# A fixed sequence of operations in place of a planner, and pairs of units in the second half of an attention kernel

## The chip, the cores and the metric

The kernel runs on one core of a Trainium2 chip. The metric is the device time of one execution in microseconds; the kernel before takes 975.54 us (median of 3 runs, 974.77 to 976.95). TensorE (PE) multiplies matrices, VectorE (DVE), ScalarE (ACT) and GpSimd (POOL) work on elements, and SyncE (SP) issues the DMAs.

## What is computed

A causal attention with a cumulative bias is followed by two feed-forward layers. All tensors are float32; the data of q and k are scaled by 8 before the call, which changes no shape.

```python
B, H, S, D = 4, 8, 576, 64
scores = q @ k.T / sqrt(D)                       # causal
bias   = -(cum[:, :, :, None] - cum[:, :, None, :])   # cum = cumsum(max(s, 0))
attn   = softmax(scores + minimum(bias, 0)) @ v
x = attn.transpose(0, 2, 1, 3).reshape(B * S, H * D)          # 2304 x 512
h = x @ moe_w_in                                 # 512 -> 2048
x = (h - tanh(h)) @ moe_w_out                    # -> 512
x = ((x @ moe2_w_a) * (x @ moe2_w_b)) @ moe2_w_out   # 512 -> 1536 -> 512
```

## The kernel before, in words

Precision comes from splitting each float32 factor into a high and a low 16-bit part; every such matrix is scaled by a power of two first, which needs its norm. So an operand of a product is loaded, squared and summed (ACT), summed over the partitions by a product with ones (PE), turned into a power of two by a handful of one- to three-column operations (DVE, `pow2`), and then split into hi (a scaled copy) and lo (the scaled difference).

**Attention.** A *unit* is one batch, one pair of heads and one half of the queries. The first half (`u.merged` false) holds the query tiles 0 and 1 of 128 rows. The second half (`u.merged` true, 16 units) holds tiles 2 and 3 and the last 64 rows, the *tail*; the tails of the two heads share one tile. A unit goes through `g_load` (raw q, k, v into SBUF, DMAs on SP), `u_load` (bias rows into `kB`), `g_square`, `g_scale`, `g_split` (v), `u_split` (q and k into tile `qk`), `u_turn` (one DMA transpose of `qk` into `qkT`, then copies into `kB`, `qB`, `qkT`), the products q·k, the exponentials, and the products with v. In the first half several units share a group `g` and so a load, a scale and a split of v; in the second half each unit is its own group. Its tile `raw` has two buffers (`BUFS_R`), `qk` one, `v` three.

**The layers.** Rows go through the first layer in 8 blocks of 256 rows and one tail block: per block eight tiles `h`, then `g` and its hi and lo (`ghl`), and a sum in `acc`. Its blocks run between attention units, since each needs finished attention rows. The second layer comes last, from about 650 us of the profile on; most of its blocks use seven products in place of eight, with sums of half tiles before them (`sq<-sq`, `g<-g`, `w<-sq,g`, 128x256).

**What sets the order.** The program records every operation with what it depends on, and the engines on which it may run (`either`: DVE, ACT or POOL). `follow` gives each operation a due time, decoded from the string `ORDER`. `run` then simulates the engines with a table of costs (`cost`), issues what is ready and due first, and picks the engine that would be done first. A POOL instruction that reads two tiles waits for the DVE instruction of that sort which was issued last before it. Nearly every instruction passes one helper, so all have the line L651 (L635 in the changed kernel); tiles tell them apart.

Of the kernel before, what the change touches and what calls it, by code (L numbers as in the profile page):

```python
# [38 lines left out]
    "Ibs7IAzUIANqIAOkIAOKIAPbIARiIATLIAU6IAWOIAsGIAV6IAUdIAaJIAeJIAlVIAoSIAbpIAdbIAezIAh4IAjWIAgtIAe4IAelIAPWIARyIAOHIATBIAUP"  # L39
    "IAQlIAOQIAUiIAVuIAYeIAZnIAbxIAePIAcrIAXFIARtIAYLIARJIAaCIAZ/IAGLIAgTIAmpIAVyIAZgIAZDIAX8IAUmIAm8IAkOIAjbIAklIApsIApXIApQ"  # L40
    "IAlhIAhBIAoeIAoHIAnoIAuBIA1YIAqJIAu1IA88IAp9IAn7IAiFIAkOIAo/IAqPIAl5IAkPIArzIAweIAqfIAv6IBCUIA2yIBL0IAtNIAiGIAqhIAsqIAwa"
    "IAm+IArHIA05IAz0IAyLIAzdIAydIA3+IA8dIA/pIBBrIBCuIBAxIBCFIBPCIBFqIBHkIBHoIA7JIA78IBHlIA5dIA6sIA5eIBBuIBEPIBDxIBMCIBF/IBFO"
    "IBHdIBTNIBSuIAg3IAc2IAbnIAeVIAeyIAf6IAd6IAZWIAUrIAceIAdHIAYwIAh0IAh+IAiDIAlCIAmSIAsLIAt6IAm9IArnIAobIAv3IAl/IAn2IApVIAlD"
    "IAs2IAxvIBBhIBAMIBFqIBI3IA2eIBDxIA4LIBBlIBBrIA8YIBDQIBFEIBHRIBFTIBJzIBWZIBElIBJ2IBDnIBDpIBECIBEDIBGUIBIcIBIbIBPNIBKrIBMS"
    "IBZKIBa7IBcNIAxeIA3MIBFKIAzrIA84IA+HIBA1IBGPIA92IBF5IBIFIBMvIBNJIBR/IBPjIBLzIBLNIBT8IBTZIBFOIBSBIBPmIBQ4IBTUIBRYIBOLIBP9"
    "IBPYIBQOIBRiIBWRIBYXIBZIIBD0IBWpIBWrIBdJIB2XIEPgIEf8IEPZID9jICmLICq+ICVJICaLICZ1ICWlICdoIAx8IA2KIA4tIA62IAw4IBG9IBLLIBMa"
    "IApPIAwtIA0vIBDYIBS+IBenIBfpIB8wIBbfIBWWIBhaIBjRIBc6IB/IIB7fIB9uIBeCIB0yIBzkIB+tIB01IB7fIB+CICGeIBz0ICDpICExICLcICR2ICXs"
    "ICZuIClOICXKICjpICniIC0xIB6FICHoICWfIC8+ICK7ICg9ICcPIC6+IC+KIDKZIDNDIDPXIDBjIDRGIDUzIDWaIDWiIDXTIDZyIDdNIBOuIBm3IBhCIBgN"
    "IBgpIBzBIBuiIBy5IBQ5IBp4IBUqIBoEIBiuIBktIB4eICAeIB0pICBEIB5/IB/2ICIMICJzICOJICGjICHjICNEICLNICPoICLeICMiICcVICgrICVCICZZ"
    "ICWdICoaICxZICytICr2IC7PIC+dIC/RIDAuIDDwIDElIDHtIDONIDSBIDIXIDMFIDJkIDKOIDQiIDTQIDY+IDcvIDeCIDe/IDiRIDj7IDltIDmIIEA0IDln"  # L50
# [12 lines left out]
    "IEDOIEFiID7jID97ID7MID5vID+tIEIiIEKxIESLIEJNIEKgIEBtIEIPIEGGIEHRIEGRIERqIEVcIEVqIEaKIEgeIEQaIEZvIEQsIEVkIEcqIElzIEhyIEnQ"
    "IEkTIEiXIEXpIEdcIEY7IEc3IEk+IEopIEoCIEsXIEzTIE6qIEqoIErZIEuUIEw5IEywIE3xIE5vIE+xIE/lIFDAIE3yIFBzIE8pIFBPIFN5IFNrIFOuIFSt"
    "IFXLIFhhIFGEIFHvIFMfIFORIFaaIFYaIFXiIFcmIFdJIFoJIFahIFVYIFW3IFXiIFZGIbptIFcLIFclIFWnIFagIF+EIClDICeUICr4ICt5IC1IIC5BICt4"
    "IC4uIDCAIDRQIDTDIDUNIDW9IDVuIDW6IDZvIDcHIDb6IDgwIDbFIDb+IDn3IDCVIDbBIDhRIDYWIDiCIDenIDhBIDqYIDp0IDsxIDw/ID03ID2/IDwZID2G"
# [144 lines left out]
AHEAD = 20e3  # L211
# [125 lines left out]
class Plan:  # L337
# [133 lines left out]
    def follow(self, order):  # L471

        if 4 * len(self.ops) != len(order):
            return
# [1349 lines left out]
```

## Time and profile before

| what | value |
|---|---|
| median of 3 runs | 975.54 us |
| profiled execution | 976.21 us |
| its span | 974.4 us (1.8 us lie around it) |
| mean granted clock of TensorE | 0.991 |
| PE busy | 897.3 us, 92% |
| DVE busy | 787.2 us, 81%, 2056 instructions |
| ACT busy | 553.3 us, 57%, 1118 instructions |
| POOL busy | 180.4 us, 19%, 297 instructions |

Busy time is the union of the instructions on an engine; a stage that is bound by an engine shows it busy nearly all of the stage. The stages used below are the stretches between the first products of certain blocks: up to 41 us nothing of the first layer can run, from 130 us on attention and the first layer run interleaved, the second half of the queries is loaded from 202 us on, and from 650 us on the second layer runs alone.

### The profile page before, as it was taken

The page shows a single profiled execution, that of the slowest core. Times are in us where ns is not written, and L with a number is a line of the kernel's source. Part 1 is how long each engine was busy: PE and PEld are TensorE (multiplying, and loading weights), DVE is VectorE, ACT ScalarE, POOL GpSimd, SP SyncE. Part 2 cuts the span into 40 slices and gives each one's busy share as a digit, 9 for nine tenths or more (in the row PEclk, how much of TensorE's full clock was granted, in tenths as well). Part 3 has the DMA queues.
Part 4 walks back from the last instruction along what each step waited for, and adds up shares of the span by engine and source line. Part 5 has one row for each costly group of instructions (what it writes and reads, how often), then busy time and mean ns, then how long its engine had stood idle before and what let it go on. Part 6 is the DMA issues. An engine that isn't in the chain of part 4 may idle for free.

```text
span 974.4 us, 19580 instructions
## 1 busy us (share of the span) xinstructions
PE 897.3 (92%) x7304; PEld 617.2 (63%) x7304; DVE 787.2 (81%) x2056; ACT 553.3 (57%) x1118; POOL 180.4 (19%) x297
## 2 busy tenths in 40 slices
PE   1587988999998999999989999999999999999998
PEld 0354656666565656666656677686777777777774
DVE  8999998969999999998899999994585466466454
ACT  6888776748778788787798854431222122222220
POOL 2123122304344343322000022020020001000000
PEclk9998989999999999999999999999999999999999
DMA  8999964458999888888755410100020011000001
GB/s 227 190 296 246 219 129 84 97 100 156 167 180 180 165 177 159 183 167 140 273 195 194 152 44 23 44 1 23 10 79 2 1 44 45 1 1 17 28 1 44
DMA packets 262304, 109.16 MB, mean 112 GB/s; under 512 B 235264, under 2 KB 243696, under 8 KB 262208
## 3 DMA queue, kind: packets, MB, share of 16 engines
q1 hardware_dynamic: 262208, 107.90, 48.2%
q8 instruction: 57, 0.93, 0.4%
q14 instruction: 39, 0.32, 0.1%
HBM read 55.81 MB, written 11.17 MB: 69 GB/s over the span
## 4 chain that ended last, share of the span: by engine, by line
PE 51%; DVE 14%; DMA 6%; ACT 5%; issue 3%; SPq 2%; POOL 0%; ACTq 0%; DVEq 0%; POOLq 0%
PE h L651 16%; PE qk L651 14%; PE acc L651 13%; PE pv L651 8%; DMA qkT<-qk 3%; SPq L651 2%; DVE qk L651 2%; DVE a L651 2%; DVE ghl L651 1%; DVE w L651 1%; DVE h L651 1%; DMA raw<-in_k_dram 1%; DVE xf L651 1%; DVE z L651 1%; ACT sq L651 1%
## 5 line engine op out<-in xcount | busy, mean ns | idle before, releaser
L651 PEld LDWEIGHTS <-w 128*128 128x128 f16 x3840 | 372.0, 98 | 81.2 <-issue 9.5
L651 PE MATMUL h<-xhl,w 128*128 128x256 f16 x2256 | 280.9, 273 | 8.0 <-DVE ghl L651 2.6
L651 PE MATMUL acc<-w,ghl 128*128 128x512 f16 x984 | 234.4, 380 | 4.7 <-DVE ghl L651 3.1
L651 PEld LDWEIGHTS <-ghl 128*128 128x128 f16 x1128 | 108.2, 98 | 121.6 <-DVE ghl L651 7.0
L651 PE MATMUL h<-xf,w 128*128 128x256 f16 (+1 forms) x416 | 71.8, 311 | 0.0
L651 DVE CUSTOM_DVE_ANT_0 qk<-qk,caus,cs 128x128 f32<-128x128 f32 (+3 forms) x120 | 64.8, 554 | 2.5 <-PE qk L651 2.4
L651 ACT ACTIVATE g<-h 128x512 f32<-128x512 f32 x38 | 22.4, 596 | 66.0 <-PE h L651 63.7
L651 PE MATMUL qk<-qkT 128*128 128x128 f16 (+4 forms) x168 | 45.8, 316 | 13.8 <-DVE qkT L651 6.0
L651 DVE TENSOR_TENSOR sq<-sq 128x256 f32<-128x256 f32 x44 | 18.6, 422 | 47.3 <-ACT sq L651 47.3
L651 PE MATMUL pv<-xf,w 128*128 128x256 f16 x432 | 55.3, 273 | 1.3 <-DVE xf L651 0.9
L651 PE MATMUL qk<-xf,w 128*128 128x256 f16 x432 | 54.8, 273 | 0.0
L651 ACT ACTIVATE th<-h,xc 128x512 f32<-128x512 f32 x64 | 43.8, 685 | 15.4 <-PE h L651 13.1
L651 ACT ACTIVATE w<-w 128x1024 f32<-128x1024 f32 (+1 forms) x42 | 47.8, 1167 | 2.4 <-DMA w<-in_moe_w_out_dram 2.1
L651 PEld LDWEIGHTS <-sq 128*128 128x128 f16 x288 | 28.2, 98 | 31.0
L651 PEld LDWEIGHTS <-v 128*64 128x64 f16 x1440 | 37.9, 112 | 13.9 <-issue 12.4
L651 PE MATMUL qk<-kB,qB 67*128 67x128 f16 (+4 forms) x168 | 45.5, 314 | 0.0
L651 PEld LDWEIGHTS <-qkT 128*128 128x128 f16 (+1 forms) x176 | 16.7, 102 | 41.1 <-DVE qkT L651 17.0
L651 ACT ACTIVATE sq<-pv 128x512 f32<-128x512 f32 x24 | 14.3, 597 | 49.2 <-PE pv L651 49.0
L651 ACT ACTIVATE w<-h,cpc 128x256 f32<-128x256 f32 x24 | 11.3, 473 | 53.2 <-PE h L651 53.1
L651 DVE TENSOR_TENSOR g<-g 128x256 f32<-128x256 f32 x48 | 19.7, 429 | 26.9 <-ACT g L651 26.7
L651 ACT ACTIVATE sq<-raw 128x576 bf16<-128x576 f32 (+2 forms) x57 | 38.4, 675 | 5.2 <-DMA raw<-in_q_dram 2.4
L651 PE MATMUL pv<-aT,v 128*64 128x128 f16 x960 | 35.0, 224 | 4.4 <-DMA aT<-a 2.7
(267 smaller groups left out, 1728.1 us busy)
## 6 DMA issues: line engine op xcount, KB each, us to landing
w<-in_moe_w_out_dram SPq DMA_DIRECT2D x8, 1024.0 KB
w<-in_moe_w_in_dram SPq DMA_DIRECT2D x6, 1024.0 KB
x_d<-sq SPq DMA_DIRECT2D x9, 512.0 KB
w<-in_moe_w_a_dram SPq DMA_DIRECT2D x4, 1024.0 KB
out_dram<-x2f SPq DMA_DIRECT2D x16, 256.0 KB
ws<-in_moe_w_out_dram SPq DMA_DIRECT2D x3, 1024.0 KB
xf<-in_moe_w_b_dram SPq DMA_DIRECT2D x3, 1024.0 KB
w<-in_moe_w_b_dram SPq DMA_DIRECT2D x3, 1024.0 KB
```

The costliest lines, as they stand in the source:

```text
L651: return getattr(getattr(plan.nc, name), what)(*[real(a) for a in args], **{k: real(a) for k, a in kw.items()})
```

## The change

It does two things. `ORDER` no longer holds due times but the finished sequence: three characters for each operation, its index and the number of the engine that it runs on. A new function `emit` issues the operations in that sequence, with the same rule between POOL and DVE, and the simulation isn't run. (Two constants of the cost table are changed too; `emit` doesn't read them.)

Second, the units of the second half form pairs. `raw` gives way to `rawq`, `rawk` and `rawv`, each of one buffer for two units; `v` has two buffers of a pair in place of three of a unit. The loads of a pair are 11 DMAs in place of 18, each of twice the size. Norm, ones product and `pow2` are made once for a pair, so two units share their scales. The hi parts of q and k and both parts of v are written for the pair by one instruction each; the lo parts of q and k, the transpose and all that follows stay by unit. The tail rows move between the heads in the tiles (`wq`, `wk`, `qat`).

```diff
 ORDER = (
-    "Ibs7IAzUIANqIAOkIAOKIAPbIARiIATLIAU6IAWOIAsGIAV6IAUdIAaJIAeJIAlVIAoSIAbpIAdbIAezIAh4IAjWIAgtIAe4IAelIAPWIARyIAOHIATBIAUP"
...
-BUFS_R = {"raw": 2, "qk": 1, "z": 1, "inv": 4, "v": 3, "a": 3, "am": 1, "aTm": 1}
+BUFS_R = {"rawq": 1, "rawk": 1, "rawv": 1, "qk": 1, "z": 1, "inv": 4, "v": 2, "a": 3, "am": 1, "aTm": 1}
...
     def follow(self, order):
-        if 4 * len(self.ops) != len(order):
-            return
-        for op in self.ops:
-            t = base64.b64decode(order[4 * op.seq:4 * op.seq + 4])
-            op.dl = 8.0 * (int.from_bytes(t, "big") - (1 << 21))
+        if 3 * len(self.ops) == len(order):
+            n = [A64.index(c) for c in order]
+            n = [n[i] << 12 | n[i + 1] << 6 | n[i + 2] for i in range(0, len(n), 3)]
+            self.steps = [(self.ops[i >> 2], i & 3) for i in n]
+
+    def emit(self, switch):
+        if not self.steps:
+            return self.run(switch)
+        self.begin()
+        for op, way in self.steps:
+            assert all(p.wait < 0 for p in op.pred)
+            op.wait = -1
+            op.eng, op.fn, op.dur, op.lag = op.alts[way]
...
+            made = op.fn()
+            if op.fn.lock and op.eng == "vector":
+                self.turn = made
+            elif op.fn.lock and self.turn is not None:
+                self.after(made, self.turn)
...
-            if u.merged or p % (PAIRS if j == 0 else NP) == 0:
+            if p % (PAIRS if j == 0 or u.merged else NP) == 0:
                 u.g = Group()
...
             if u.merged:
-                far = 0 if nm == "q" else FAR
...
-                for h in range(2):
-                    pl.sync.dma_start(
-                        t[:, h * nt + far:(h + 1) * nt, :],
-                        src[u.b, 2 * u.p + h, (t0 + far) * P:(t0 + nt) * P, :].rearrange("(t p) d -> p t d", p=P))
+                t = anew(u, [P, 2 * n * w, D], F32, "raw" + nm)
...
+            heads = src[u.b, 2 * u.p:2 * (u.p + n)]
+            far = FAR if u.merged and nm != "q" else 0
+            if far:
+                pl.sync.dma_start(
+                    t.rearrange("p (h t) d -> p h (t d)", t=w)[:, :, 0:far * D],
+                    heads[:, 0:far * P, :].rearrange("h (p t) d -> p h (t d)", t=far))
+            for x in range(far, nt):
+                pl.sync.dma_start(
+                    t.rearrange("p (h t) d -> p t h d", t=w)[:, x],
+                    heads[:, (t0 + x) * P:(t0 + x + 1) * P, :].rearrange("h p d -> p h d"))
+            if u.merged:
+                i = u.b * NP + u.p
+                pl.sync.dma_start(
+                    t.rearrange("p (r x) d -> p r x d", r=n)[:, :, nt, :],
+                    tail_d[i:i + n, :, "qkv".index(nm), :].rearrange("r p d -> p r d"), reads=["tail"])
...
+    def split(t, raw, sc, flat=False):
+        copy_scaled(t[:, :, :, 0, :], raw, sc)
+        for x in [slice(None)] if flat else [slice(i, i + 1) for i in range(t.shape[1])]:
+            lo_part(t[:, x, :, 1, :], raw[:, x], sc, t[:, x, :, 0, :])
...
     with tc.manual_schedule():
         pl.follow(ORDER)
-        pl.run(switch)
+        pl.emit(switch)
```

Between the two programs the instructions of the engines change as follows: PE 14322 to 14306 (counting weight loads), DVE 2058 to 1835, ACT 853 to 798, POOL 302 to 488, SP 401 to 345 (these counts leave out the accumulator reads that the profile lists by themselves). The raw loads of the second half fall from 144 to 88.

The first place is SP's queue at the first loads of the second half (`raw` is a unit's tile, `rawq`, `rawk` and `rawv` are a pair's; the number behind a name is a tile's own). Before:

```order
L651 DMA raw_2583<-in_k_dram 128x2x64 x2
L651 DMA raw_2583<-in_v_dram 128x2x128
L651 DMA raw_2583<-tail_d 128x3x64
L651 DMA raw_2583<-in_v_dram 128x2x64
L651 DMA raw_2583<-in_q_dram 128x2x64 x2
L651 DMA raw_2583<-in_v_dram 128x2x64
L651 DMA raw_2583<-in_k_dram 128x2x128
L651 DMA raw_2659<-in_q_dram 128x2x64
L651 DMA raw_2659<-in_v_dram 128x2x128
```

After:

```order
L635 DMA rawv_2607<-in_v_dram 128x4x64
L635 DMA rawk_2643<-in_k_dram 128x4x64 x2
L635 DMA rawv_2607<-in_v_dram 128x4x64
L635 DMA rawv_2607<-tail_d 128x2x64
L635 DMA rawv_2607<-in_v_dram 128x4x128
L635 DMA rawk_2643<-in_k_dram 128x4x128
L635 DMA rawk_2643<-tail_d 128x2x64
L635 DMA rawq_2691<-in_q_dram 128x4x64 x2
L635 DMA rawq_2691<-tail_d 128x2x64
L635 DMA kB_2739<-part_d 3x1152
L635 DMA kB_2749<-part_d 3x1152
```

Nine loads of a unit, followed at once by the next unit's, have become 11 loads of a pair, after which come the bias rows (`kB`) of its two units.

The second place is ACT's queue just behind: `sqs` receives the sums of squares, `sc` holds the scales, `th` and `ghl` belong to the first layer. Before:

```order
L651 ACTIVATE sq_2668,sqs_2669<-raw_2583 128x320
L651 ACTIVATE sq_2674,sqs_2669<-raw_2583 128x576
L651 ACTIVATE sq_2684,sqs_2669<-raw_2583 128x576
L651 ACTIVATE qk_2729<-raw_2583,sc_2726 128x9x64
L651 ACTIVATE v_2740<-raw_2583,sc_2726 128x9x64
L651 ACTIVATE sq_2750,sqs_2751<-raw_2659 128x576
L651 ACTIVATE sq_2764,sqs_2751<-raw_2659 128x320
L651 ACTIVATE th_2782<-h_2689,xc_1_2312 128x512
L651 ACTIVATE sq_2790,sqs_2751<-raw_2659 128x576
L651 ACTIVATE ghl_2802<-h_2689,xsg_2364 128x512
```

After:

```order
L635 ACTIVATE sq_2673,sqs_2674<-rawv_2607 128x1152
L635 ACTIVATE sq_2693,sqs_2674<-rawk_2643 128x1152
L635 ACTIVATE sq_2710,sqs_2674<-rawq_2691 128x640
L635 ACTIVATE qk_2754<-rawk_2643,sc_2751 128x2x9x64
L635 ACTIVATE th_2781<-h_2656,xc_1_2225 128x512
L635 ACTIVATE ghl_2799<-h_2656,xsg_2358 128x512
L635 ACTIVATE v_2816<-rawv_2607,sc_2751 128x18x64
```

Six squares for two units have become three of twice the width, and the hi copies are twice as wide too.

The third place is in the second layer (last block but one), where half tiles are added ahead of the seven products. On DVE before:

```order
L651 TENSOR_TENSOR sq_12090<-sq_12090 128x256
L651 TENSOR_TENSOR g_12105<-g_12105 128x256
L651 TENSOR_TENSOR g_12120<-g_12120 128x256
L651 TENSOR_TENSOR w_0_171<-sq_12090,g_12120 128x256
L651 TENSOR_TENSOR sq_12143<-sq_12143 128x256
L651 TENSOR_TENSOR w_0_171<-sq_12143,g_12105 128x256
L651 TENSOR_TENSOR w_0_171<-pv_12063,g_12120 128x512
L651 TENSOR_TENSOR w_0_171<-h_12077,w_0_171 128x256
L651 TENSOR_TENSOR w_0_171<-qk_12124,g_12105 128x512
L651 SCALAR_TENSOR_TENSOR w_0_171<-w_0_171,cpc_8595 128x768
```

On DVE after, and then on POOL after:

```order
L635 SCALAR_TENSOR_TENSOR w_0_137<-w_0_137,cpc_8339 128x768
L635 TENSOR_SCALAR sq_11954<-pv_11941 128x512
L635 TENSOR_TENSOR w_0_137<-sq_11954,g_11937 128x256
L635 TENSOR_TENSOR w_0_137<-h_11883,w_0_137 128x256
L635 TENSOR_TENSOR w_0_137<-qk_11896,g_11912 128x512
L635 TENSOR_TENSOR w_0_137<-pv_11941,g_11937 128x512
```

```order
L635 TENSOR_TENSOR g_11912<-g_11912 128x256
L635 TENSOR_TENSOR sq_11920<-sq_11920 128x256
L635 TENSOR_TENSOR g_11937<-g_11937 128x256
L635 TENSOR_TENSOR sq_11954<-sq_11954 128x256
L635 TENSOR_TENSOR w_0_137<-sq_11920,g_11912 128x256
L635 TENSOR_TENSOR ghl_11826<-w_0_137,ghl_11826 128x512
```

The sums `g<-g` and `sq<-sq`, and every other `w<-sq,g` here, have moved from DVE to POOL, and a copy `sq<-pv` out of PSUM has moved from ACT to DVE.

## Rows read from the trace of the kernel before

**Rows 1.** Busy us by stage: window, length, PE, PEld, DVE, ACT, POOL (x instructions), PEclk, DMA, GB/s.

```profile
0.00:41.00 41.00, 9.47 (x75) 6.28 (x76) 36.02 (x145) 31.20 (x77) 9.85 (x25) 1.00 0.90 213
41.00:130.00 89.00, 73.83 (x350) 44.81 (x349) 82.27 (x242) 70.89 (x134) 20.44 (x27) 0.92 0.95 230
130.00:231.00 101.00, 93.07 (x775) 62.61 (x773) 85.57 (x297) 70.57 (x179) 29.83 (x63) 1.00 0.55 112
231.00:428.00 197.00, 186.66 (x2015) 120.92 (x2015) 186.50 (x570) 158.42 (x361) 77.99 (x133) 1.00 0.89 169
428.00:482.00 54.00, 52.96 (x540) 35.42 (x538) 47.53 (x133) 38.63 (x71) 8.61 (x16) 1.00 0.83 198
482.00:572.00 90.00, 85.38 (x598) 57.62 (x596) 87.39 (x192) 76.27 (x107) 8.30 (x10) 0.98 0.49 166
572.00:650.00 78.00, 75.67 (x594) 57.82 (x593) 77.89 (x147) 35.28 (x71) 10.85 (x8) 1.00 0.12 31
650.00:975.00 325.00, 320.22 (x2371) 231.72 (x2368) 184.06 (x339) 72.10 (x127) 14.48 (x16) 1.00 0.07 22
```

**Rows 2.** What PE waits for in 41:130 us: total us, times, longest us.

```profile
PE acc L651 <- DVE g L651: 4.5, 3, 2.6
PE pv L651 <- ACT sq L651: 3.6, 2, 2.3
PE qk L651 <- ACT zs L651: 2.4, 2, 1.4
```

**Rows 3.** The same in 130:650 us.

```profile
PE pv L651 <- DVE p2n L651: 3.5, 2, 3.2
PE acc L651 <- DVE ghl L651: 3.1, 5, 1.4
PE qk L651 <- ACT zs L651: 2.9, 5, 1.0
PE h L651 <- DVE ghl L651: 2.6, 5, 0.9
PE h L651 <- DVE g L651: 1.9, 2, 1.4
```

**Rows 4.** Chain that ends last in 231:428 us, shares by engine and line.

```profile
by line: DMA qkT<-qk 11.7%; issue 8.6%; DVE qk L651 6.6%; DVE a L651 6.1%; PE acc L651 5.2%; PE h L651 5.1%; SPq L651 4.9%; DMA raw<-in_k_dram 4.0%; DVE z L651 3.2%; ACT sq L651 2.8%; DVE h L651 2.8%; DVE ghl L651 2.7%; ACT qk L651 2.4%; DM
```

**Rows 5.** SP issues on tile raw, 200:500 us: ns min/median/max, first to last start.

```profile
L651 SPq DMA_DIRECT2D raw<-in_k_dram x48: 378/468/1258, 202.4 to 413.2; - x48
L651 SPq DMA_DIRECT2D raw<-in_v_dram x48: 450/469/1927, 203.3 to 417.6; - x48
L651 SPq DMA_DIRECT2D raw<-in_q_dram x32: 368/469/1438, 205.2 to 412.6; - x32
L651 SPq DMA_DIRECT2D raw<-tail_d x16: 529/552/615, 203.9 to 412.0; - x16
```

**Rows 6.** SP transposes into qkT, 200:540 us, same columns.

```profile
L651 SPq DMA_TRANSPOSE qkT<-qk x16: 1441/1642/3938, 214.7 to 432.6; - x16
```

**Rows 7.** ACT squares of raw, shapes apart: busy us, mean ns, idle before.

```profile
L651 ACT ACTIVATE sq<-raw 128x576 bf16<-128x576 f32 x32 | 21.6, 677 | 2.7 <-DMA raw<-in_v_dram 1.6 <-DMA raw<-in_k_dram 0.7
...
L651 ACT ACTIVATION_READ_ACCUMULATOR sq<-raw 128x1 f32 x57 | 10.9, 192 | 0.0
...
L651 ACT ACTIVATE sq<-raw 128x1024 bf16<-128x1024 f32 x9 | 9.4, 1049 | 0.0
...
L651 ACT ACTIVATE sq<-raw 128x320 bf16<-128x320 f32 x16 | 7.4, 461 | 2.4 <-DMA raw<-in_q_dram 2.4
```

**Rows 8.** DVE, shapes apart, same columns.

```profile
L651 DVE TENSOR_TENSOR g<-g 128x256 f32<-128x256 f32 x48 | 19.7, 429 | 26.9 <-ACT g L651 26.7
...
L651 DVE TENSOR_SCALAR p2a<-p2n 128x3 int32<-128x3 int32 x21 | 3.4, 160 | 0.2
```

**Rows 9.** POOL, shapes apart, same columns.

```profile
L651 POOL TENSOR_TENSOR sq<-sq 128x256 f32<-128x256 f32 x4 | 2.9, 728 | 75.8 <-ACT sq L651 67.0 <-DVE sq L651 7.7 <-DVE th L651 1.0
```

**Rows 10.** DVE on tile sq: ns min/median/max, first and last start.

```profile
L651 DVE TENSOR_TENSOR w<-sq,g x44: 411/424/1000, 632.5 to 951.9; 128x256 f32<-128x256 f32 x44
```

More of the change, by code (lines that the diff above doesn't have):

```diff
@@ L1 @@
-import base64
 import heapq
@@ L351, in __init__ @@
         self.turn = None
+        self.steps = []
         self.shift = {}
@@ L471, in follow @@
     def follow(self, order):
-        if 4 * len(self.ops) != len(order):
-            return
-        for op in self.ops:
-            t = base64.b64decode(order[4 * op.seq:4 * op.seq + 4])
-            op.dl = 8.0 * (int.from_bytes(t, "big") - (1 << 21))
+        if 3 * len(self.ops) == len(order):
[10 more added lines that the diff above has]
+            op.eng, op.fn, op.dur, op.lag = op.alts[way]
+            for b in op.bufs:
+                if b.real is None:
+                    assert self.usable(b.pool, switch)
+                    b.real = self.open[b.pool].tile(
+                        b.shape, b.dtype, tag=b.tag, name=b.name, bufs=self.tags[b.pool, b.tag]["bufs"])
+            made = op.fn()
[3 more added lines that the diff above has]
+                self.after(made, self.turn)
+            for b in op.bufs:
+                b.left -= 1
+                self.unused[b.pool] -= not b.left
     def run(self, switch=None):
@@ L705, in cost @@
         if what == "dma_start_transpose":
-            return 650.0, 1600.0, b / 266.0
-        hold = 475.0 if b < 2e4 else 630.0 if b < 9e5 else 560.0
+            return 650.0, 1600.0, b / 242.0
+        hold = 475.0 if b < 2e4 else 636.0 if b < 9e5 else 560.0
         return hold, 910.0 if b < 1e6 else 2000.0, b / (180.0 if main.shape[-1] * size < 512 else 360.0)
@@ L993, in g_load @@
         u, n = g.lead, len(g.units)
-        slots = [n * u.sq, n * u.sk, n * u.sk]
-        if n == PAIRS:
-            raw = ws()[:, 0:sum(slots) * D].bitcast(F32).rearrange("p (s d) -> p s d", d=D)
-        else:
-            raw = anew(u, [P, sum(slots), D], F32, "raw")
-        g.raw = {}
+        g.raw = {}
+        what = (("q", q, u.ts[0], u.nq, u.wq), ("k", k, 0, u.nk, u.wk), ("v", v, 0, u.nk, u.wk))
+        if not u.merged:
+            slots = [2 * n * w for _, _, _, _, w in what]
+            if n == PAIRS:
+                raw = ws()[:, 0:sum(slots) * D].bitcast(F32).rearrange("p (s d) -> p s d", d=D)
+            else:
+                raw = anew(u, [P, sum(slots), D], F32, "raw")
@@ L1030, in g_square @@
     def g_square(g):
-        g.sqs = anew(g.lead, [P, 3], F32, "sqs")
+        u = g.lead
+        g.sqs = anew(u, [P, 3], F32, "sqs")
         for i, nm in enumerate("qkv"):
-            junk = new("moe", [P, 1024], BF16, "sq", 2)
-            raw = g.raw[nm].rearrange("p a d -> p (a d)")
-            pl.scalar.activation(
-                out=junk[:, :raw.shape[1]], in_=raw, func=AF.Square, accum_out=g.sqs[:, i:i + 1])
+            junk = new("moe", [P, PAIRS * (2 * NT + 1) * D], BF16, "sq", 2)
+            raw = g.raw[nm]
+            if u.merged:
+                raw = raw.rearrange("p r x d -> p r (x d)")
+                junk = junk[:, 0:raw.shape[1] * raw.shape[2]].rearrange("p (r x) -> p r x", r=raw.shape[1])
+            else:
+                raw = raw.rearrange("p r x d -> p (r x d)")
+                junk = junk[:, :raw.shape[1]]
+            pl.scalar.activation(out=junk, in_=raw, func=AF.Square, accum_out=g.sqs[:, i:i + 1])
     def small(what, **kw):
@@ L1202, in u_pv @@
                     for h in range(2):
-                        sl = 2 * NT if kt == NT else h * NT + kt
+                        sl = NT if kt == NT else h * u.wk + kt
                         todo.append((
```

316 lines of the change are left out of this document (140 added, 176 removed).

## The prediction

> **What bounds the kernel now.** I read the table of busy time by stage first, then the list of what PE waits for, then the chain that ends last, then the queues. The table [rows 1] shows PE busy 320.22 of the last 325 us and 186.66 of 197 between 231 and 428 us: over most of the program the work of PE itself is the bound, and the change hardly touches it (16 of 14322 instructions go). So all that an edit beside PE can give is PE's idle time, length minus busy time of each row: 31.5 us up to 41 us, 15.2 up to 130, 7.9 up to 231, 10.3 up to 428, 1.0 up to 482, 4.6 up to 572, 2.3 up to 650, and 4.8 after it, 77.7 in all. Where is it open to this change? Up to 41 us the first loads and norms fill DVE (36.02 busy); the changed order keeps that work. The 15.2 us up to 130 us stand against DVE's `g`, ACT's `sq` and `zs` [rows 2], while DMA is busy for 0.95 of the stage. From 130 to 650 us the first entries are DVE's `p2n`, `ghl` and `g` and ACT's `zs` [rows 3]: operations that came late in a queue that was full, since DVE is busy 186.50 of 197 us between 231 and 428 us and 77.89 of 78 before 650 [rows 1]. A second candidate is SP: the chain between 231 and 428 us gives 11.7% to the transposes into `qkT`, 4.9% to SP's queue and 4.0% to the loads of k [rows 4].
>
> **SP and the loads.** The 144 loads of single units take 48, 48 and 32 times 0.47 us and 16 times 0.55 [rows 5], 69 us of SP between 202 and 418 us, a third of that stretch. The 88 after are 64 of q, k and v and 24 of tails: 30.0 + 13.2 = 43 us if an issue of twice the size costs the same. 26 us of queue go; if an issue cost twice as much, 64 x 0.47 = 30 us would come back and nothing was won, which is the bad end. The maxima of 1.3 to 1.9 us in the same rows are such cases, but the medians hold. I take the 26. On the path it is worth a part only: SP's own share of the chain is 4.9% of 197 us = 9.7 us, and the bytes stay the same. DMA is busy 0.89 of that stage [rows 1], 175 us; the stage can't fall under that, so up to 22 us are open there.
>
> **ACT.** The squares of the second half cost 32 x 0.677 + 16 x 0.461 + 48 x 0.192 = 38.2 us [rows 7]. Between 576 and 1024 columns the price rises by 0.372 us, 0.83 ns a column, so 1152 columns are some 1.16 us and 640 some 0.73: 16 x 1.16 + 8 x 0.73 + 24 x 0.192 = 29.0. That is 9 us less; both ends of this lie within 2 us. ACT is busy 158.42 of 197 us, so this counts only where a square is late.
>
> **DVE and POOL.** Eight chains of `pow2` go: five operations of 0.16 us each [rows 8] and five smaller ones, together 6 to 12 us on DVE and POOL. More comes from the sequence, which puts other engines to work. DVE falls by 223 instructions. Some 82 of them are sums and steps of the second layer, where DVE is busy 184 of 325 us and not the bound; the other 141 lie before 650 us, where 603 us of DVE [rows 1] are 1726 instructions, 0.35 us each: 49 us or 8% less DVE time before 650 us. POOL gets 186 more. At the mean price of its 297 (180.4 us by the rows' sum, 0.61) that is 113 us; before 650 us POOL was busy 166 us (the sum of its column, [rows 1]), so it has room. What it costs: a sum of 256 columns takes 0.728 us on POOL [rows 9] against 0.429 on DVE [rows 8], 0.30 us longer. In the second layer 24 `g`, 18 `sq` and 18 `w` sums move; PE never waits 0.3 us for one there as long as a block's sums are made ahead of it, and 320.22 of 325 us say that they are. I cost it at nothing; the cover is the finished tiles ahead of PE, and if it went and the 24 sums of one kind showed, it would be 24 x 0.3 = 7 us.
>
> **Reading of two tiles by POOL beside DVE.** The sum `w<-sq,g` on DVE takes 0.424 us in the median and 1.000 at worst [rows 10]: sometimes it is held by 0.58 us. The Trainium skill (SBUF — State Buffer, Who interferes with whom) says that a DVE instruction with two SBUF inputs contends with a POOL instruction that reads SBUF, and that the loser waits for the whole instruction. By that rule, more POOL work returns some of the DVE time that it frees; the row agrees that single instructions are held, but its median lies only 0.013 above its minimum. So few are: I take nothing, and the other end is a rival below.
>
> **Pairs as a loop.** With one buffer for `rawq`, `rawk` and `rawv`, the next pair's loads can't start before this pair's hi and lo parts are made. Before, 16 units were loaded from 202 to 418 us [rows 5]: 27 us for two. The first unit needs 12.3 us from its first load (202.4) to its transpose (214.7), the last 15.0 from its last load (417.6) to its transpose (432.6) [rows 5, 6]. A pair has in addition 5 us of issues (11 x 0.47), 2 us of wider squares and some 4 us of wider copies and second lo parts: 19 to 26 us of the 27 that it has. That just fits, so I cost it at nothing; it is the thinnest cover of this change. The second unit of a pair has its operands earlier than before, which helps.
>
> **The sum**, against the profiled execution of 976.2 us:
> - Between 130 and 482 us PE idles 7.9 + 10.3 + 1.0 = 19.2 us. The named releasers are late DVE and ACT work and SP's loads, and DVE loses 8%, ACT 9 us, SP 26 us. I take 60% away: 11.6. The ends are none (the last waits get a new releaser) and all 19.2.
> - Between 482 and 650 us it idles 6.9 us, and DVE stays the bound (87.39 of 90 and 77.89 of 78 busy); a third: 2.3.
> - Between 41 and 130 us 15.2 us; the changed sequence only reorders the work of the first half, and DMA is at 0.95. A fifth: 3.0.
> - Up to 41 us and after 650 us: nothing.
>
> 16.9 us together give 959.3 for the profiled run. The median of the runs lies 0.7 below the profiled one, so I forecast 958.6, rounded to 959.
>
> **Rivals.**
> 1. *PE's idle time only changes its releaser.* For it: waits are spread over a score of entries with none above 3.5 us [rows 3], and taking one away often shows the next a little later. Against: DVE and SP are both relieved in the same stage. Then the time is that of before to within 2 us, 975.
> 2. *Part of the gain is lost to bytes or to the two readers.* DMA at 0.89 to 0.95 lets the loads land no earlier. Or POOL holds DVE: if each of the 104 extra POOL instructions before 650 us holds a DVE instruction for half of its 0.61 us, 31 of the 49 us come back, and 18/49 of the 16.9 remain, 6 us: 970. Each of the two has about half of this rival's chance; that single sums are held up to 0.58 us speaks for the second [rows 10], their median against it. The rule of the Trainium skill quoted above (SBUF — State Buffer) is this second one.
> 3. *Slower: the loop of pairs.* Place: 230 to 430 us. If a pair takes longer than the 27 us that PE leaves it, each of the seven that follow the first comes later by the excess. It decides from 27 us on; at 29 us it is 7 x 2 = 14 us and no gain there: 976 + 14 = 990. For it: the upper bound of 26 us above, and SP holds its queue in order, so a load that waits for a buffer also holds the transposes behind it, 1.6 us each [rows 6]. Against: what the order shows, where the loads of the next pair stand ahead of the transposes only where its buffer is free early.
> 4. *More than that.* In 41 to 130 us the granted clock is 0.92 [rows 1], so PE runs a sixth of the time at 1.2 instead of 2.4 GHz; with a closer order there the clock would hold. All 19.2 us, half of the 15.2 and 7 us of clock (0.08 x 89) give 976 - 34 = 942.
>
> **How the numbers follow.** A difference of 0.2%, 2 us, is about what a measurement of this kernel can tell. Forecast (948 to 967): 0.50. Rival 1: 0.13. Rival 2 (967 to 973): 0.11. Rival 3 (978 to 1000): 0.18. Rival 4 (under 948): 0.08. Faster is 0.50 + 0.11 + 0.08 = 0.69, within 0.2% 0.13, slower 0.18. The range leaves out the lower part of rival 4 (0.06) and the upper two thirds of rival 3 (0.13): 945 to 983.
>
> **What would show it.** In the profile after: PE's idle time from 130 to 482 us at about 8 us where it was 19; from 650 us on PE still busy all but 5 of its 325 us, though POOL does 60 more sums there (else my cover was wrong); DVE some 80 us less busy, POOL over 110 more; SP with gaps between its issues from 230 us on; a median of 0.47 us for a load of twice the size. If the list of PE's waits names `qkT` or `kB` and q·k products between 230 and 430 us, rival 3 is at work; if the median of `w<-sq,g` on DVE rises from 0.42 us, rival 2. The prediction is wrong if the first 130 us or the last 325 change by more than 5 us, which I hold to be fixed.

## The result, and the profile after

The changed kernel takes 947.45 us (median of 4 runs, 946.18 to 948.67) against 975.75 us before (4 runs), a ratio of 0.9709 with a 95% interval of 0.9692 to 0.9726: 28.3 us faster. The prediction said 959 with a range of 945 to 983. The direction and the range hold. The gain is 1.7 times the 16.9 us of the sum and ends 0.5 us below the 948 to 967 of the forecast, in what stood as rival 4; and 11.7 us of it are made ahead of the second block, in a stretch whose length the prediction held to be fixed. The profiled execution after has a span of 945.5 us.

The first view is busy time by stage of the kernel after (window, length, PE, PEld, DVE, ACT, POOL with instructions, granted clock, DMA share, GB/s). Its windows begin at the first product of the blocks that begin the windows of [rows 1], so that line answers to line; the seventh window ends where 325 us are left, as there.

```profile
0.00:41.20 41.20, 9.84 (x74) 5.60 (x75) 34.98 (x139) 34.50 (x83) 14.49 (x35) 1.00 0.96 230
41.20:118.80 77.60, 69.99 (x350) 44.18 (x350) 73.17 (x214) 69.92 (x129) 20.48 (x39) 0.96 0.95 241
118.80:213.20 94.40, 94.22 (x780) 63.65 (x777) 82.88 (x273) 76.72 (x186) 48.22 (x82) 1.00 0.69 136
213.20:404.80 191.60, 186.38 (x2020) 121.51 (x2021) 174.54 (x495) 165.73 (x323) 108.14 (x153) 1.00 0.95 179
404.80:453.40 48.60, 45.08 (x503) 31.69 (x502) 38.40 (x104) 31.76 (x61) 12.77 (x19) 0.99 0.73 163
453.40:545.00 91.60, 88.95 (x611) 59.03 (x612) 85.95 (x194) 79.81 (x113) 19.46 (x20) 0.98 0.55 180
545.00:620.50 75.50, 75.08 (x593) 57.58 (x592) 70.72 (x130) 30.08 (x62) 11.74 (x13) 1.00 0.13 35
620.50:945.50 325.00, 320.94 (x2375) 231.79 (x2373) 173.90 (x292) 47.25 (x86) 115.74 (x126) 1.00 0.08 20
```

In the last 325 us PE is busy 320.94 us where it was 320.22. (That this window is as long as before follows from where it is cut; the table of block starts below shows it independently, with 346.7 and 346.6 us from the second layer's block 2 to the end.) The first window is 41.2 us where it was 41, with 31.4 us of PE idle where it was 31.5. All of the gain lies between. The second window is 77.6 us where it was 89: PE idles 7.6 us of it, half of the 15.2, and is busy 3.8 us less for the same number of products, with its clock granted 0.96 and not 0.92. From 118.8 to 453.4 us PE idles 0.2 + 5.2 + 3.5 = 8.9 us where it was 19.3, and the next two windows have 3.1 where it was 6.9. Over the span DVE is busy 734.5 us (787.2 before) and POOL 351.0 (180.4).

What PE waits for after, between 41 and 119 us (total us, times, longest us), answers to [rows 2]; behind it the same between 119 and 620 us, for [rows 3].

```profile
PE pv L635 <- ACT sq L635: 2.4, 2, 1.3
PE qk L635 <- DMA kB<-part_d: 1.6, 1, 1.6
PE qk L635 <- DVE a L635: 1.5, 2, 1.1
PE acc L635 <- DVE g L635: 1.1, 3, 0.4
```

```profile
PE h L635 <- DVE ghl L635: 4.3, 3, 3.5
PE pv L635 <- ACT sq L635: 3.2, 4, 1.3
PE acc L635 <- DVE sq L635: 0.7, 1, 0.7
```

In the first list DVE's `g`, the greatest entry of before with 4.5 us, has 1.1; in the second nothing but one wait for `ghl` of 3.5 us and the squares is left over 1 us, and the `p2n`, `zs` and `g` of before are gone. The only transfer in the whole list of before between 41 and 130 us are the transposes into `aT`, its fourth entry:

```profile
PE pv L651 <- DMA aT<-a: 2.1, 2, 1.7
```

How waits cost twice in the early stage shows in rows of PE's timeline (start, length, product; the idle time before it in brackets). The eight products with the third tile `g` of block 1, first before, then after, where they are two rows:

```profile
74.13 5.40 PE L651 MATMUL acc<-w,g 128*128 128x512 f32 x8 [2.62 <-DVE g L651]
```

```profile
67.98 1.99 PE L635 MATMUL acc<-w,g 128*128 128x512 f32 x4 [0.34 <-DVE g L635]
69.83 1.96 PE L635 MATMUL acc<-w,g 128*128 128x512 f32 x4
```

Before, PE was busy 7.5 of the 10.1 us ahead of these products, and they took 5.40 us, at a granted clock of 0.68 in the mean (its two levels are 1.2 and 2.4 GHz, so it was at the lower one for part of them). After, it was busy 9.6 of the 9.9 us ahead, and they took 3.95 us at 1.00. So 1.45 us of slower products come on top of the wait. It is not the last wait alone that counts. The eight products with the fifth tile, before and after:

```profile
93.79 5.40 PE L651 MATMUL acc<-w,g 128*128 128x512 f32 x8 [1.02 <-DVE g L651]
```

```profile
86.18 6.04 PE L635 MATMUL acc<-w,g 128*128 128x512 f32 x8 [0.40 <-DVE g L635]
```

After, they come behind a wait of only 0.40 us and are slow all the same (granted clock 0.60): in the 10.1 us ahead of them PE was busy 5.9 us, with several short waits. Here the change gained nothing.

SP's loads of the second half of the queries answer to [rows 5] (ns min/median/max, first to last start):

```profile
L635 SPq DMA_DIRECT2D rawq<-in_q_dram x16: 377/500/1083, 187.8 to 371.4; - x16
```

```profile
L635 SPq DMA_DIRECT2D rawk<-in_k_dram x24: 403/506/1467, 184.0 to 379.5; - x24
L635 SPq DMA_DIRECT2D rawk<-tail_d x8: 467/506/1068, 187.2 to 379.0; - x8
```

The squares on ACT answer to [rows 7] (busy us, mean ns, idle time before and its releasers), the sums on DVE and POOL to [rows 8 to 10]:

```profile
L635 ACT ACTIVATE sq<-rawv 128x1152 bf16<-128x1152 f32 x8 | 9.3, 1162 | 6.7 <-DMA rawv<-tail_d 3.0 <-issue 2.0 <-DMA rawv<-in_v_dram 1.7
...
L635 ACT ACTIVATE sq<-rawq 128x640 bf16<-128x640 f32 x8 | 5.8, 729 | 0.6 <-DMA rawq<-tail_d 0.6
```

```profile
L635 DVE TENSOR_TENSOR g<-g 128x256 f32<-128x256 f32 x24 | 12.5, 524 | 6.3 <-ACT g L635 6.2
...
L635 DVE TENSOR_TENSOR w<-sq,g 128x256 f32<-128x256 f32 x26 | 11.2, 429 | 5.2 <-POOL sq L635 3.8 <-POOL g L635 1.1
...
L635 DVE TENSOR_SCALAR p2a<-p2n 128x3 int32<-128x3 int32 x13 | 2.7, 211 | 0.4
```

```profile
L635 POOL TENSOR_TENSOR g<-g 128x256 f32<-128x256 f32 x24 | 19.4, 807 | 67.7 <-DVE sq L635 30.9 <-DVE g L635 25.5 <-ACT g L635 4.4
...
L635 POOL TENSOR_TENSOR sq<-sq 128x256 f32<-128x256 f32 x22 | 17.2, 784 | 42.3 <-ACT sq L635 21.4 <-DVE sq L635 10.8 <-DVE xf L635 5.8
```

A load of twice the size takes SP 0.50 us in the median where one of a unit took 0.47. Added up one by one, the 88 raw loads hold SP for 51.5 us where the 144 held it for 84.4; both sums lie above the medians times the counts, since single issues take over 1 us. The wide squares take 1.16 and 0.73 us, just as the prediction worked out from narrower ones. Sums of half tiles on POOL take 0.78 to 0.81 us, a little more than the 0.728 of [rows 9].

### The profile page after: what moved, and what is told of

Read it like the earlier page. It is cut to its first block, busy times and chain, and to the rows that moved or that the text cites. A ratio compares the mean times of both kernels' runs of the same rounds, so it can differ in the third digit from the quotient of the medians.

```text
span 945.5 us, 19496 instructions
## 1 busy us (share of the span) xinstructions
PE 890.5 (94%) x7296; PEld 615.0 (65%) x7296; DVE 734.5 (78%) x1833; ACT 535.8 (57%) x1039; POOL 351.0 (37%) x483
## 4 chain that ended last, share of the span: by engine, by line
PE 54%; ACT 4%; DVE 4%; issue 2%; DMA 1%; SPq 1%; ACTq 0%; DVEq 0%
PE h L635 17%; PE qk L635 15%; PE acc L635 14%; PE pv L635 8%; DMA rawv<-tail_d 1%; ACT w L635 1%; ACT sq L635 1%; SPq L635 1%; DVE ghl L635 1%; DVE qk L635 1%; ACT th L635 1%; ACT xf L635 0%; ACT ghl L635 0%; DVE h L635 0%; DVE xhl L635 0%
## 5 line engine op out<-in xcount | busy, mean ns | idle before, releaser
L635 PE MATMUL acc<-w,ghl 128*128 128x512 f16 x984 | 230.9, 379 | 1.3 <-DVE sq L635 0.7
L635 ACT ACTIVATE g<-h 128x512 f32<-128x512 f32 x26 | 15.5, 595 | 76.3 <-DVE w L635 40.2
L635 PEld LDWEIGHTS <-v 128*64 128x64 f16 x1440 | 37.6, 113 | 12.1 <-issue 11.7
L635 POOL TENSOR_TENSOR g<-g 128x256 f32<-128x256 f32 x24 | 19.4, 807 | 67.7 <-DVE sq L635 30.9
L635 ACT ACTIVATE sq<-pv 128x512 f32<-128x512 f32 x16 | 9.5, 597 | 60.1 <-PE pv L635 33.9
L635 DVE SCALAR_TENSOR_TENSOR h<-h,xc,th 128x512 f32<-128x512 f32 x48 | 36.1, 752 | 5.9 <-ACT th L635 5.7
L635 DVE SCALAR_TENSOR_TENSOR ghl<-h,xsg,ghl 128x512 f16<-128x512 f32 x48 | 35.8, 745 | 3.9 <-ACT ghl L635 3.5
L635 ACT ACTIVATE qk<-qk,nm 128x512 f32<-128x512 f32 (+1 forms) x56 | 31.7, 566 | 7.4 <-DVE nm L635 6.3
L635 DVE SCALAR_TENSOR_TENSOR a<-qk,sm,a 128x512 f16<-128x512 f32 (+1 forms) x56 | 35.2, 630 | 0.7 <-ACT a L635 0.4
```

Of the source, the lines that this page charges most:

```text
L635: return getattr(getattr(plan.nc, name), what)(*[real(a) for a in args], **{k: real(a) for k, a in kw.items()})
```

## The experiments

A fixed sequence can be taken apart: each operation of one program has a counterpart in the other (an operation of a pair has two, one for each unit), so a kernel can keep the operations of one program and take the places, or the engines, or both, from the other, for all operations or for some. An operation whose buffer is not free yet in such a sequence is put behind the one that frees it. `ORDER` is then a new string of the same code, of which the diffs show the first characters at most. The times of all these kernels are medians; the kernel before took 974.6, 974.6 and 975.7 us beside the three series.

The table gives, for most of them, when the first product `h` of a block starts in its profile (us). The blocks do not stand at quite the same place of the attention work in the two sequences, so single rows are good to a few us. The row "second layer" is its first `h`; at 571.7 us before, it begins ahead of the 650 us from which it runs alone.

| start of | before | after | early | late | no pairs | pairs, old | by unit | one raw | POOL back |
|---|---|---|---|---|---|---|---|---|---|
| block 1 | 41.0 | 41.2 | 41.1 | 41.1 | 42.1 | 41.0 | 41.6 | 41.7 | 44.3 |
| block 2 | 130.5 | 118.8 | 121.2 | 128.2 | 120.6 | 129.3 | 118.8 | 120.3 | 121.7 |
| block 3 | 187.0 | 169.4 | 177.8 | 178.4 | 171.9 | 186.3 | 169.9 | 170.8 | 176.1 |
| block 4 | 231.2 | 213.2 | 221.4 | 222.3 | 221.6 | 241.1 | 218.3 | 217.8 | 225.4 |
| block 5 | 301.4 | 280.6 | 290.0 | 289.9 | 301.8 | 324.3 | 291.7 | 291.0 | 298.4 |
| block 7 | 427.6 | 404.8 | 415.6 | 413.3 | 448.3 | 480.2 | 426.5 | 421.5 | 431.9 |
| block 8 | 482.1 | 453.4 | 470.5 | 461.9 | 497.4 | 534.0 | 475.3 | 470.2 | 482.4 |
| second layer | 571.7 | 545.0 | 560.7 | 555.1 | 589.7 | 624.0 | 567.2 | 562.2 | 580.2 |
| its block 2 | 627.7 | 598.9 | 616.7 | 609.0 | 643.5 | 680.0 | 621.1 | 616.1 | 635.8 |
| end of the span | 974.4 | 945.5 | 963.4 | 955.6 | 989.9 | 1026.7 | 967.8 | 962.5 | 981.7 |

Of the 28.9 us between the two spans, 17.6 are there at block 3. After, block 3 begins at 169.4 us, and SP issues the first load of a pair at 183.5 us; the kernel without pairs, the next one, has 15.1 us of gain at that row too. So the greater part of the gain is made ahead of the pairs, by the sequence and its engines. The other 11 us lie where pairs run.

**The two things apart.** First the sequence of after without pairs (the kernel before, with `emit`, a new `ORDER` and these lines):

```diff
-BUFS_R = {"raw": 2, "qk": 1, "z": 1, "inv": 4, "v": 3, "a": 3, "am": 1, "aTm": 1}
+BUFS_R = {"raw": 2, "qk": 2, "z": 1, "inv": 8, "v": 4, "a": 3, "am": 1, "aTm": 1, "sqs": 4, "sc": 4, "cs": 4}
...
-        pl.run(switch)
+        pl.emit(switch)
```

> The units of the second half load, scale and split alone again (144 loads), but every operation stands where its counterpart stands in the sequence of after, on the engine that it has there. Small tiles and v and qk get as many buffers as two pairs and one pair have, so that no buffer is shorter than in after. Theory A (the gain of 28 us comes from the sequence and the engines): most of it is kept, 947 to 956 us. Theory B (it comes from the pairs: 26 us of SP's queue, 9 us of ACT, some 10 of DVE): less than half is kept, 962 to 976.

Measured: 989.47 us, 15 us slower than before and 42 slower than after. Neither theory holds. By the table nothing is lost up to block 3 (171.9 against 169.4 us), and 41 us are lost from there to block 7, while the second half is loaded. The wait list of PE there (total us, times, longest) says why:

```profile
PE pv L713 <- ACT sq L713: 14.6, 9, 3.8
PE pv L713 <- DMA aT<-a: 5.9, 2, 4.8
```

ACT's own list there (170 to 475 us) begins with

```profile
ACT sq L713 <- DMA raw<-in_v_dram: 13.8, 5, 4.3
ACT sq L713 <- DMA raw<-in_q_dram: 8.3, 4, 4.2
```

The products with ones wait for squares, and those for loads: the chain of a unit starts late. Two things that this kernel puts back are priced one by one below: more and smaller loads (23 us) and raw data in one tile that comes free as a whole (16.7 us). Together they have the size of the 42 us; that they add up is not shown.

And the pairs without the sequence, which is the kernel after with another `ORDER`:

```diff
 ORDER = (
-    "AAIABkAAMABsABwAAEACAAAAAAQAAUAB4AAYAAcAAgAAkAAsAAwAA0ABEABJABNABSABoAB8"
+    "AAMAAEAAIAAAABsABkAB4AAQABoAAUABwAAYAB0AAcAAgAAkAH0AAsAAoAAwAA8AA0ABAAHw"
...
```

> The pairs alone: the operations of after in the sequence of before, with the engines of before; an operation of a pair stands where the first unit's stood. Theory A (sequence and engines): 968 to 980 us, pairs alone give under a third of the gain, or even lose since the second unit's loads and splits come too early. Theory B (pairs): 948 to 961.

Measured: 1029.44 us, 55 us slower than before: beyond both theories. The loss is again made between block 3 and block 7, and PE waits there for the same thing:

```profile
PE pv L704 <- ACT sq L704: 26.7, 6, 6.8
PE pv L704 <- ACT xf L704: 11.1, 1, 11.1
PE qk L704 <- DVE a L704: 5.4, 1, 5.4
```

So, taken over as they stand and for the whole program, both halves of the change lose without the other. A run in which the order is free to adapt says the same for the pairs. With an empty `ORDER` the planner runs on rough due times, once with the operations of before, once with those of after:

```diff
-ORDER = (
...
-)
+ORDER = ""
```

> The kernel before with an empty ORDER: the planner orders the operations by its rough due times alone, as units. It is the partner of the next run; on its own it shows what the decoded due times gave: 985 to 1040 us.

> After with an empty ORDER, so that the same planner with its rough due times orders the pairs. Against the run before it this is the pairs' worth where the order adapts to them. Theory B (a pair takes 24 us less of SP's queue and about 20 less of ACT and DVE, in a stretch where SP's queue showed for 23 of 30 us): 10 to 25 us faster than its partner. Theory A (pairs are worth something only in a sequence made for them): within 5 us of its partner, or slower.

Measured: 1045.71 us for the units (above the 985 to 1040 expected; the decoded due times of before are worth 70 us) and 1056.32 us for the pairs: 10.6 us slower, as theory A had it. These planner runs also leave POOL nearly unused: 133 and 125 us busy.

**The early part.** Next, the sequence of after only ahead of the second block, in the kernel before:

```diff
-        pl.run(switch)
+        pl.emit(switch)
```

`ORDER` then holds 718 operations with their places and engines of after, and behind them all others with those of before.

> The kernel before, units alone, with the sequence and engines of after only for what stands there ahead of the second block's first product (some 119 us of its profile); all else in the sequence of before. In the profiles the second block starts 11.7 us earlier in after (118.8 against 130.5). Theory A: that gain was made by the early sequence and stays until the end, 964 to 967 us. Rival: what comes next is bound by DVE or DMA, and the gain is given back by 230 us: 972 to 977.

Measured: 963.05 us (ratio 0.9879, 0.9862 to 0.9896), 11.5 us faster, a little more than theory A expected. Block 2 starts at 121.2 us where it was 130.5, and the gain is there at the end. PE's waits between 41 and 122 us:

```profile
PE qk L713 <- DVE a L713: 2.5, 2, 1.7
PE pv L713 <- ACT sq L713: 2.4, 2, 1.3
...
PE acc L713 <- DVE g L713: 0.8, 2, 0.4
```

The waits for DVE's `g` have become short here too, as in after. As many bytes as before pass ahead of block 2, 29.22 MB, in 121.2 us in place of 130.5, with DMA busy 0.98 of them. The early sequence moves DMAs as well, and that may have a share in the gain: before, ACT and DVE themselves waited for weights between 41 and 130 us (ACT 2.1 us for `w` and 0.9 for `ws`; DVE 1.7 for `ws`, 1.4 and 0.7 for `w`), and in the early run their lists have no such entry. The runs do not separate the order of the loads from that of the small operations.

The counterpart is the kernel after with only `ORDER` changed: what stands ahead of block 2 has the places and engines of before, all behind it those of after.

> After, with pairs, but what stands ahead of the second block's first product keeps the sequence and the engines of before; everything behind it stands as in after. The early part alone gave 11.5 us (963.1). If the two parts add up, this kernel gives the rest: 957 to 961 us. Rival: the late part is tuned to what the early part leaves behind (which buffers and engines are free when), and breaks without it: 965 us or more.

Measured: 957.78 us, 16.8 us faster than before. This is as expected if the parts add up: 11.5 + 16.8 = 28.3 us, the whole gain. The early part holds no pairs yet, so 11.5 us have nothing to do with them. Is it the order there, or the engines? The next kernel is the early run with only the engine numbers in `ORDER` changed: each operation runs where it does in before, which differs for 82 of the 718.

> The kernel before with the sequence of after for what stands there ahead of the second block (718 operations), as in the run that gave 963.1 us, but now with the engines of before throughout (82 of the 718 differ). Theory A1 (the sequence alone makes the early gain): 962 to 966 us. Theory A2 (the sequence and its engines belong together, as the run with all engines put back showed): 968 us or more.

Measured: 985.76 us: 10 us slower than before, 23 slower than with its engines. PE's list up to 145 us shows what happens where an operation comes at a place that was meant for another engine:

```profile
PE pv L713 <- ACT sq L713: 13.6, 5, 6.7
PE qk L713 <- DVE qkT L713: 7.2, 4, 4.6
PE acc L713 <- DVE a L713: 7.2, 5, 2.2
```

So the order alone loses. What the engines of after give in the order of before is not known.

**The loads.** In after, each load of q, k and v split in two of half the size:

```diff
-            heads = src[u.b, 2 * u.p:2 * (u.p + n)]
...
+            whole = t
+            for r in range(n if u.merged else 1):
+                m = 1 if u.merged else n
+                t = whole[:, 2 * r * w:2 * (r + m) * w] if u.merged else whole
+                heads = src[u.b, 2 * (u.p + r):2 * (u.p + r + m)]
...
```

> After, with each load of q, k and v of a pair issued as two of half the size (152 loads in place of 88; the tail rows stay by pair), everything else the same. Theory B1 (the 26 us of SP's queue matter): the 64 issues of 0.47 us, 30 us of SP, show for a good part between 180 and 400 us, 955 to 972 us. Theory B2 (SP had room, and the pairs help by fewer norms and squares and by their buffers): 947 to 951 us.

Measured: 970.40 us, 23 us slower than after. The operations and bytes are the same; 64 issues more, 30 us of SP by the price of 0.47 us, show for three quarters. Between 170 and 475 us PE and then ACT wait for (total us, times, longest us):

```profile
PE pv L707 <- ACT sq L707: 14.4, 8, 3.3
```

```profile
ACT sq L707 <- DMA rawv<-in_v_dram: 6.7, 3, 3.2
...
ACT sq L707 <- DMA rawv<-tail_d: 5.4, 4, 2.1
...
ACT sq L707 <- DMA rawk<-in_k_dram: 2.8, 4, 1.7
```

The squares wait for the data, and PE's product with ones for the squares: 14.4 us where after has 3.2. PE is slower as well: from block 3 to block 7 it idles 17.8 us where it idles 5.3 in after, and it is busy 238.8 us in place of 230.1, at a granted clock of 0.97 in place of 1.00. So theory B1 holds: in this sequence the number of SP's issues is a bound of this stage. Whether two loads of half the size also land later than one is not separated.

**The loop of pairs.** In after, the three raw tiles as one of the same size:

```diff
-BUFS_R = {"rawq": 1, "rawk": 1, "rawv": 1, "qk": 1, "z": 1, "inv": 4, "v": 2, "a": 3, "am": 1, "aTm": 1}
+BUFS_R = {"raw": 1, "qk": 1, "z": 1, "inv": 4, "v": 2, "a": 3, "am": 1, "aTm": 1}
...
-                t = anew(u, [P, 2 * n * w, D], F32, "raw" + nm)
+                if nm == "q":
+                    one = anew(u, [P, 2 * n * sum(x[4] for x in what), D], F32, "raw")
+                t = one[:, o:o + 2 * n * w, :]
+                o += 2 * n * w
```

> After, with rawq, rawk and rawv made one tile of the same size with one buffer, so that the next pair's first load has to wait for the last split of q, k and v (in the sequence, 8 operations move by over 20 places for that). Theory C1 (the loop of pairs has little room, as the prediction's rival 3 says; it fits only since the three tiles come free one by one): 953 to 975 us. Theory C2 (it has room): 947 to 950 us.

Measured: 964.19 us, 16.7 us slower than after. What ACT's squares and PE wait for:

```profile
ACT sq L704 <- DMA raw<-tail_d: 12.8, 7, 3.8
```

```profile
PE pv L704 <- ACT sq L704: 8.8, 5, 2.1
```

Theory C1 holds: the loop of pairs fits into the time that it has because each raw tile is loaded anew as soon as its own split is done. What two buffers of each raw tile would give is not known.

**The engines.** All operations of after that exist in both programs on the engines of before, then only those that went from DVE to POOL ahead of 600 us, then all that stand behind 600 us, whichever engine they came from. The edit is in the two low bits of the steps in `ORDER`, which name the engine: 596, 123 and 204 of them change, and no place does.

> After, in its sequence, but wherever an operation exists in both programs it runs on the engine that it has in before (596 of 4171 change it; most of what moved to POOL goes back to DVE). Theory A1 (the sequence is what counts, the engines not): 947 to 952 us. Theory A2 (the relief of DVE counts: 8% of its time before 650 us): 955 to 970.

> After in its sequence, but the 123 operations ahead of 600 us that moved from DVE to POOL go back to DVE; moves to and from ACT stay. With the prediction's price of 0.35 us for a DVE instruction and one to three instructions each, DVE gets some 50 us of work more in 600. Theory: DVE is the next bound there, and about half of that shows: 965 to 985 us. Rival: DVE had room in after (it is 95% busy or less in each stage): 947 to 953.

> After, with the engines of before for all that stands in the sequence behind 600 us (204 operations; the half-tile sums go back from POOL to DVE), in the sequence of after. The prediction costs the move to POOL at nothing since finished tiles cover it: 945 to 949 us. Rival: with the sums on DVE the fixed sequence lets DVE fall behind, or POOL's sums had relieved it: 951 us or more.

Measured: 1059.73, 984.54 and 955.03 us. The first is 112 us slower than after, far outside both theories: with the engines changed the sequence is no better than the planner's rough one. The second is 37 us slower, at the upper end of its theory. Between 41 and 620 us PE waits there (total us, times, longest us) for

```profile
PE h L704 <- DVE ghl L704: 12.1, 12, 3.7
PE qk L704 <- DVE a L704: 6.1, 9, 1.9
...
PE acc L704 <- DVE sq L704: 4.6, 6, 1.4
```

and its busy time between 231 and 428 us (columns as above) is

```profile
231.00:428.00 197.00, 180.60 (x1898) 115.15 (x1896) 183.88 (x518) 158.07 (x306) 47.59 (x74) 0.99 0.86 169
```

with POOL at 47.6 us where after has some 108, and DVE at 183.9. The third loses 7.6 us, in the stretch where the prediction costed the move at nothing:

```profile
PE h L704 <- ACT g L704: 3.1, 3, 1.6
PE h L704 <- DVE g L704: 1.8, 1, 1.8
```

PE waits for half tiles that ACT copies and DVE adds; in after its list there has one entry, of 0.2 us.

## Why the prediction was right, and where its sizes were off

1. **PE's idle time as the measure: right, with one term left out.** The idle time fell by 22.7 us (77.7 to 55.0, the sums of length minus busy time), and PE was also busy 6.8 us less (897.3 to 890.5). The clock's share, some 4 us in the early stage (0.08 x 89 before, 0.04 x 77.6 after), stood in rival 4 only; a wait that goes takes the slow products behind it along, as the rows of the third tile `g` show, and belonged in the sum.
2. **41 to 130 us: mis-sized.** The sum took a fifth of 15.2 us, 3.0, since "the changed sequence only reorders the work of the first half, and DMA is at 0.95". It gave 11.5 us (the early run); in after, 7.6 us less of idle and 3.8 us less of busy time of PE. The step that failed is to take DMA at 0.95 for a bound. The early run passes the same bytes in 9.3 us less, and PE's list of before [rows 2] has its great entries at `g`, `sq` and `zs`, thus at the order and the engines of small operations, with one transfer of 2.1 us; what loads cost beside that went through ACT and DVE, 6.8 us of their waits for weights. This one stage makes 8.5 of the 11 us that the forecast missed. The prediction called itself wrong if the first 130 us changed by more than 5 us; they changed by 11.7, so by this sign it was wrong about the stage.
3. **130 to 482 us: right within its ends.** 60% of 19.2 us were taken, 11.6; the idle time there fell by 10.4 us, to 8.9 where "about 8" had been named. Measured against block 8 the gain from 118.8 us on is 17.0 us (28.7 less 11.7), of which the rest is busy time of PE (and work that stands on the other side of the cut in the new sequence). The late run gave 16.8. Between 482 and 650 us a third of 6.9 us was taken, 2.3, and 3.9 of idle time went.
4. **SP's queue: the relief was right, its worth on the path probably too low.** 26 us were to go; with 0.50 us an issue it is 88 x 0.50 = 44 in place of 69, 25 us; by the sums of all issues 33 us (84.4 to 51.5). The prediction gave at most SP's share of the chain, 9.7 us, to the path. Putting 64 issues back cost 23 of 30 us. But this price is one in a sequence that was made for 88 loads, so it is rather an upper bound.
5. **The loop of pairs: the right place for the doubt.** It was "the thinnest cover", costed at nothing, and it held; taking away the separate release of the three tiles costs 16.7 us. What decided was a detail that the prediction's 19 to 26 us did not use: the three tiles come free one by one.
6. **DVE and POOL: right in sign, mis-sized.** DVE fell by 52.7 us, not 80, and POOL rose by 170.6 where over 110 was forecast. The failed step is to price the net count of 223 instructions at the mean: behind it DVE gave 322 operations to other engines and took 160 from them, not of the same size. The worth of the moves was greater than taken: without 123 of them the kernel loses 37 us, again in a sequence made for them.
7. **After 650 us and up to 41 us: right.** Up to block 1 it is 41.2 us where it was 41.0, and from the second layer's block 2 to the end 346.6 where it was 346.7. The cover for the moved sums held in the new sequence; that the engines of before would cost 7.6 us there was not foreseen.
8. **The rivals.** Rival 4 (more than that, under 948 us) came about in good part: of the three terms that it added up, 10.4 of 19.2 us of idle time went, all of the half of 15.2, and 4 of the 7 us of clock. It had a chance of 0.08, of which the range left out 0.06; so that 947.45 lies in the range is luck, a strip of 3 us that had 0.02. Rival 1 (only the releaser changes) and rival 3 (slower by the loop) did not come about, though the pairs in the old sequence lost 53 us in rival 3's place, between blocks 3 and 7. Of rival 2 the two readers are there on a small scale, as the last section shows.

What stays open: how fast the units would be in a sequence made for them. No run here tells, since none had such a sequence; the planner's runs say only that pairs aren't faster in a rough order. And which of the 82 engine choices matter in the early part is not known.

## What to carry to other kernels

In a program like this one, whose five queues hold all operations in an order fixed beforehand, the sequence, the engine of each operation and the buffers' shapes are one thing: taking back a part of it cost 8 to 112 us in ten kernels here, in five of them more than the whole gain, so an edit to such a kernel has to be judged with a sequence made for it. Where the list of waits names mostly small operations of other engines, a DMA share of 0.95 does not show that the stage can't be shorter; here the same bytes passed in less time. Idle time of PE is to be costed with the slower products behind it.

## What the runs showed of the hardware

Twice the size of a load raised its issue time on SP only from 0.468 to 0.500 us in the median, so fewer and larger loads relieve the queue almost in proportion: 0.61 times the issues took 0.61 times the time (51.5 of 84.4 us).

POOL and DVE slow each other. In the trace of after, the 18 sums `g<-g` on DVE that no POOL instruction overlaps take 0.419 us in the mean and 0.426 at most; the six that one overlaps take 0.841 in the mean. The longest, 1.383 us, lies beside a POOL instruction of 1.209 us that began 0.106 us before it, and ends 0.280 us after that. Of the 13 three-column `p2a<-p2n`, three take 0.328 to 0.393 us, each beside a POOL instruction, and the others 0.170 at most. Two of the runs show the same in the means. On DVE the sum `g<-g` rose from 0.429 us in the mean [rows 8] to 0.524, and the three-column `p2a<-p2n` from 0.160 [rows 8] to 0.211. With the second layer's engines put back, `g<-g` fell to 0.458 and `sq<-sq` on POOL to 0.726 (from 0.784); with the earlier work back, `p2a<-p2n` fell to 0.168, while `g<-g` stayed at 0.525. The rows (DVE, shapes apart, columns as above) are first of the run with the second layer's engines put back, then of the run with the 123 earlier operations back on DVE:

```profile
L704 DVE TENSOR_TENSOR g<-g 128x256 f32<-128x256 f32 x48 | 21.9, 458 | 13.7 <-ACT g L704 13.6
```

```profile
L704 DVE TENSOR_TENSOR g<-g 128x256 f32<-128x256 f32 x24 | 12.5, 525 | 6.3 <-ACT g L704 6.2
...
L704 DVE TENSOR_SCALAR p2a<-p2n 128x3 int32<-128x3 int32 x13 | 2.2, 168 | 0.4
```

The trace agrees with the rule of the Trainium skill (SBUF — State Buffer, Who interferes with whom), by which a DVE instruction with two SBUF inputs contends with a POOL instruction that reads SBUF, under a lock that one of them has for a whole instruction; `p2a<-p2n` reads one tile, and for such operations the same section allows contention where they run in a two-port mode, which no run here tells apart. In size it is small: for `g<-g` 24 x 0.095 = 2.3 us, for `p2a<-p2n` 0.7, where rival 2 allowed for 31 in all. An estimate over all DVE instructions that overlap one of POOL's (their time above the median of undisturbed ones of the same shape) is 17.5 us after and 10.6 before. `w<-sq,g` on DVE took 0.429 us in the mean where it was 0.435, and its median, the sign named for rival 2, is 0.425 where it was 0.424.
